# Layer scale on one core: y's big load moved to ACT's queue, x's tail cut 56 and 4, x's head rows last

## The chip, the cores and the metric

The kernel runs on one core of one Trainium2 chip. The time is the device time of one execution in microseconds, the median of several runs. The core has a matrix engine (PE), a vector engine (DVE), ACT, POOL and SP, and 16 DMA engines that move data between HBM and the on-chip memory (SBUF). SP and ACT each have a DMA queue; in this profile q1 is SP's and q10 is ACT's, and both use the same 16 DMA engines.

## The reference

```python
B, S, D = 1024, 16, 512
x, y:  normal(B, S, D) * 0.05, bf16
gamma: 1e-4 * normal(D) * 0.05, bf16

def reference(x, y, gamma):
    return x + gamma * y
```

Each of x, y and the output is 16384 rows of 512 bf16 values, 16.78 MB. So 33.56 MB are read and 16.78 MB written, and the arithmetic is one multiplication and one addition for each element.

## The kernel before

The 16384 rows are spread over 128 partitions, 128 rows of 1 KB to a partition. `BLOCKS` cuts these into three blocks of 4, 64 and 60 rows; inside a block a partition's rows lie next to each other in HBM, so that one transfer moves one unbroken run for each partition (64 KB for 64 rows). A whole y (128 KB for each partition) stays in SBUF and is turned into the output in place; x has room for 76 rows only, so its last 60 rows reuse room of earlier ones.

Nothing schedules the work: three lists at the head of the file write its order out by hand. `SP` and `ACT` are the DMA instructions of the two queues, in program order. `('y', a, b)` loads rows a to b of y, `('x', a, b, at)` loads rows of x to row `at` of x's room, `('g',)` loads gamma, `('s', a, b)` stores. `DVE` is the order of the arithmetic over the pieces of `PIECES` (8, 16, 44, 52 and 8 rows): `('m', c)` multiplies piece c of y by gamma (line 180), `('a', c)` adds x to it (line 189).

`ring` (lines 113 to 140) writes out a queue's list. Before a transfer it puts the waits that the transfer needs, and the issuing engine stands there until they are met, with all that follows in its list behind it:

- `EARLY` instructions (the first two of SP, the first of ACT) are moved to the very start of the program.
- At the position `AHEAD` each queue waits once until the transfer `HOLD`, y's rows 0 to 4, has landed. PE watches for that landing (line 147) and releases SP, ACT and DVE. So the load of x's rows 4 to 68 and of y's rows 68 to 128 on SP, and of gamma on ACT, are issued only then.
- A load of x into room that is in use waits until the additions that read it are done (`frees`). The load of x's rows 68 to 120 takes the room of rows 24 to 68 and waits for addition 2; that of rows 120 to 128 waits for addition 0, the second in DVE's order.
- The first store waits for `RELEASE`, the landing of x's rows 68 to 120 (line 157), and every store for its additions.

Gamma comes as one row of 1 KB. PE multiplies it by a column of ones (line 152), which copies it to 128 partitions, and DVE casts the result to `gamma_sb` (line 154). All multiplications read `gamma_sb`; they come after the cast on DVE. A multiplication also waits for its rows of y, an addition for its rows of x and for the multiplications before it. DVE's order is: multiply pieces 0, 1, 2; add 2, 0, 1; multiply 3, 4; add 3, 4.

Of the kernel before, what the change touches and what calls it, by code (L numbers as in the profile page):

```python
# [5 lines left out]

BLOCKS = [4, 64, 60]

PIECES = [8, 16, 44, 52, 8]


SP = [
    ('y', 0, 4),
    ('y', 4, 68),
    ('x', 4, 68, 4),
    ('y', 68, 128),
    ('x', 68, 120, 24),
    ('x', 120, 128, 0),
]
ACT = [('x', 0, 4, 0), ('g',), ('s', 4, 68), ('s', 0, 4), ('s', 68, 128)]  # L20

EARLY = (2, 1)

HOLD, AHEAD = ('y', 0, 4), (2, 1)

RELEASE = ('x', 68, 120, 24)

DVE = [('m', 0), ('m', 1), ('m', 2), ('a', 2), ('a', 0), ('a', 1), ('m', 3), ('m', 4), ('a', 3), ('a', 4)]
MULT, ADD = mybir.AluOpType.mult, mybir.AluOpType.add


def _take(sem, n, eng):


    return eng.wait_ge(sem, n).then_inc(sem, -n)  # L35


def kernel(
# [18 lines left out]
    rows = N // P  # L57
    n = len(PIECES)
    assert sum(PIECES) == rows
    starts = [sum(PIECES[:c]) for c in range(n + 1)]  # L60
    dt = xf.dtype
# [13 lines left out]
    y_sb = nc.alloc_sbuf_tensor("y_sb", [P, rows, D], dt).ap()  # L75
    x_loads = [w for w in ACT + SP if w[0] == "x"]
    y_loads = [w for w in SP + ACT if w[0] == "y"]
    stores = [w for w in SP + ACT if w[0] == "s"]
    for loads in (x_loads, y_loads, stores):
# [9 lines left out]
    s_add, s_go, s_rel, s_end, s_out = sem("s_add"), sem("s_go"), sem("s_rel"), sem("s_end"), sem("s_out")  # L89
    added = [a for kind, *a in DVE if kind == "a"]  # L90
    order = {a[0]: k for k, a in enumerate(added)}

    def meets(a, b, c, d):
        return a < d and c < b
# [4 lines left out]
    def x_at(row):  # L99
        return next(w[3] + row - w[1] for w in x_loads if w[1] <= row < w[2])  # L100
# [12 lines left out]
    def ring(eng, what, n_early, n_ahead):  # L113

        known, went = 0, False
        for k, w in enumerate(what):
            kind = w[0]
            if k == n_ahead:
                _take(s_held[eng], 1, eng)
            need = frees(w) if kind == "x" else pieces_of(w[1], w[2]) + list(w[3:]) if kind == "s" else []  # L120
            need = max((order[c] + 1 for c in need), default=0)
            if kind == "s" and not went:
                _take(s_go, 1, eng)
                went = True
            if need > known:
                eng.wait_ge(s_add, need)
                known = need
            if kind == "g":
                i = eng.dma_start(out=gamma_row, in_=gamma.unsqueeze(0)).then_inc(s_gamma, 16)
            elif kind == "x":  # L130
                to = x_sb[:, w[3] : w[3] + w[2] - w[1], :]
                i = eng.dma_start(out=to, in_=rows_of(xf, w[1], w[2])).then_inc(s_load[w], 16)
            elif kind == "y":
                r = slice(w[1], w[2])
                i = eng.dma_start(out=y_sb[:, r, :], in_=rows_of(yf, w[1], w[2])).then_inc(s_load[w], 16)
            else:
                r = slice(w[1], w[2])
                i = eng.dma_start(out=rows_of(of, w[1], w[2]), in_=y_sb[:, r, :]).then_inc(s_out, 16)
            if k < n_early:
                early.append(i.ins)  # L140

    ring(nc.sync, SP, EARLY[0], AHEAD[0])
    ring(nc.scalar, ACT, EARLY[1], AHEAD[1])

# [11 lines left out]

    _take(s_load[RELEASE], 16, nc.tensor)
    nc.tensor.sem_inc(s_go, 1)
# [4 lines left out]
    def need(loads, c):  # L163
        for w in loads:
            if w not in landed and meets(starts[c], starts[c + 1], w[1], w[2]):
                if w == RELEASE:
                    _take(s_rel, 1, nc.vector)
                elif w == HOLD:
                    _take(s_held[nc.vector], 1, nc.vector)
                else:  # L170
                    _take(s_load[w], 16, nc.vector)
                landed.add(w)

    for kind, *args in DVE:
        c = args[0]
        yt = y_sb[:, starts[c] : starts[c + 1], :]
        if kind == "m":
            need(y_loads, c)
            g = gamma_sb[:, None, :].to_broadcast([P, PIECES[c], D])
            nc.vector.tensor_tensor(out=yt, in0=yt, in1=g, op=MULT).then_inc(s_dve, 1)  # L180
            open_mults += 1
        else:
# [4 lines left out]
            at = x_at(starts[c])  # L187
            xt = x_sb[:, at : at + PIECES[c], :]
            nc.vector.tensor_tensor(out=yt, in0=xt, in1=yt, op=ADD).then_inc(s_add, 1)  # L189
# [44 lines left out]
```

## Time and profile before

| | us |
|---|---|
| time, median of 3 runs (119.63 to 119.88) | 119.76 |
| span of the profiled execution, first to last instruction | 118.2 |
| median time less this span | 1.5 |
| DVE busy in the span | 70.1 |
| gamma's DMA issued / matmul of gamma starts | 3.90 / 11.59 |
| first multiplication starts | 23.95 |
| addition 2 starts | 43.45 |
| load of x's rows 68 to 120 issued | 55.37 |
| first store issued | 77.41 |

The profiled execution's own device time is not on the page, only its span; the row below it is the difference to the median of the timed runs. The page gives times from the first instruction. A line of the timeline reads: start, duration, engine, line of the kernel, operation, what it writes and reads, how often, and in brackets how long the engine was idle before it and what it waited for. "SPq" and "ACTq" lines are the instructions that issue a DMA; the transfer itself goes on afterwards. In the row of 40 slices each digit is the busy share of the DMA engines in tenths. Besides, the trace holds a record of every DMA packet (queue, start, duration, bytes) and the time at which each of a transfer's 16 parts reports that it has landed; where the text gives a packet's or a landing's time, it is from these.

### The profile page before, as it was taken

The page shows a single profiled execution, that of the slowest core. Times are in us where ns is not written, and L with a number is a line of the kernel's source. Part 1 is how long each engine was busy: PE and PEld are TensorE (multiplying, and loading weights), DVE is VectorE, ACT ScalarE, POOL GpSimd, SP SyncE. Part 2 cuts the span into 40 slices and gives each one's busy share as a digit, 9 for nine tenths or more (in the row PEclk, how much of TensorE's full clock was granted, in tenths as well). Part 3 has the DMA queues.
Part 4 walks back from the last instruction along what each step waited for, and adds up shares of the span by engine and source line. Part 5 has one row for each costly group of instructions (what it writes and reads, how often), then busy time and mean ns, then how long its engine had stood idle before and what let it go on. Part 6 is the DMA issues. An engine that isn't in the chain of part 4 may idle for free. (4 is left out here: it accounts for less than half of the span.)

```text
span 118.2 us, 91 instructions
## 1 busy us (share of the span) xinstructions
PE 0.6 (0%) x1; PEld 0.1 (0%) x1; DVE 70.1 (59%) x12; POOL 0.2 (0%) x4
## 2 busy tenths in 40 slices
PE   0000100000000000000000000000000000000000
PEld 0000000000000000000000000000000000000000
DVE  0000200089999969999999999999999900000000
POOL 0000000000000000000000000000000000000000
DMA  6999889988899879879969696898899889799793
GB/s 248 461 666 399 355 355 399 665 355 355 355 599 466 355 333 624 374 333 499 499 288 576 288 576 288 360 637 355 355 576 488 355 355 510 333 582 416 333 499 166
DMA packets 1442, 50.33 MB, mean 426 GB/s; under 512 B 161, under 2 KB 162, under 8 KB 546
## 3 DMA queue, kind: packets, MB, share of 16 engines
q1 hardware_dynamic: 864, 33.03, 64.8%
q10 hardware_dynamic: 578, 17.30, 33.9%
HBM read 33.56 MB, written 16.78 MB: 426 GB/s over the span
## 5 line engine op out<-in xcount | busy, mean ns | idle before, releaser
L180 DVE TENSOR_TENSOR y_sb<-y_sb,gamma_sb 128x4096 bf16<-128x4096 bf16 (+3 forms) x5 | 34.7, 6981 | 10.9 <-DVEq L35 10.9
L189 DVE TENSOR_TENSOR y_sb<-x_sb,y_sb 128x4096 bf16<-128x4096 bf16 (+3 forms) x5 | 34.7, 6981 | 1.2 <-DVEq L35 1.1
L154 DVE CAST gamma_sb<-gamma_ps 128x512 bf16<-128x512 f32 x1 | 0.7, 692 | 10.2 <-DVEq L35 10.2
L146 DVE MEMSET ones_row<- 1x128 bf16 x1 | 0.2, 165 | 2.0 <-PEq L51 2.0
L152 PE MATMUL gamma_ps<-gamma_row,ones_row 1*128 1x512 bf16 x1 | 0.6, 581 | 11.6 <-PEq L35 11.6
L152 PEld LDWEIGHTS gamma_ps<-gamma_row,ones_row 1*128 1x128 bf16 x1 | 0.1, 101 | 11.6 <-issue 11.6
L218 POOL MEMSET const-bfloat16-1.0<- 128x1 bf16 x1 | 0.1, 101 | 0.0
L218 POOL MEMSET const-uint8-127<- 128x1 uint8 x1 | 0.1, 101 | 0.0
L218 POOL MEMSET const-float32-0.0<- 128x1 f32 x1 | 0.1, 98 | 0.2 <-issue 0.2
L218 POOL MEMSET const-float32-1.0<- 128x1 f32 x1 | 0.1, 98 | 0.0
## 6 DMA issues: line engine op xcount, KB each, us to landing
y_sb<-in_y_dram SPq DMA_DIRECT2D x1, 7680.0 KB, 57.3
out_dram<-y_sb ACTq DMA_DIRECT2D x1, 7680.0 KB, 23.8
x_sb<-in_x_dram SPq DMA_DIRECT2D x1, 6656.0 KB, 21.7
x_sb<-in_x_dram SPq DMA_DIRECT2D x1, 1024.0 KB, 22.0
y_sb<-in_y_dram SPq DMA_DIRECT2D x1, 512.0 KB, 3.4
x_sb<-in_x_dram ACTq DMA_DIRECT2D x1, 512.0 KB, 4.2
out_dram<-y_sb ACTq DMA_DIRECT2D x1, 512.0 KB, 22.3
y_sb<-in_y_dram SPq DMA_DIRECT2D x1, 23.4
```

What stands on the lines that cost most here:

```text
L146: nc.vector.memset(ones_row, 1.0).then_inc(s_ones, 1)
L152: nc.tensor.matmul(gamma_ps, ones_row, gamma_row, start=True, stop=True).then_inc(s_ps, 1)
L154: nc.vector.tensor_copy(out=gamma_sb, in_=gamma_ps).then_inc(s_dve, 1)
L180: nc.vector.tensor_tensor(out=yt, in0=yt, in1=g, op=MULT).then_inc(s_dve, 1)
L189: nc.vector.tensor_tensor(out=yt, in0=xt, in1=yt, op=ADD).then_inc(s_add, 1)
L218: nc = _bacc.Bacc("TRN2", target_bir_lowering=False, num_devices=1)
```

## The change

The five lists and numbers at the head of the file change, and nothing else.

- ACT's first instruction, still moved to the start, loads y's rows 4 to 68; it was SP's second. Gamma follows it on ACT's queue, as it followed x's rows 0 to 4. Only one instruction of SP is moved to the start now, y's rows 0 to 4.
- x's rows 0 to 4 are SP's last load. They take room of x's rows 4 to 8 and wait for addition 1.
- x's last 60 rows come as rows 68 to 124, which wait for addition 2 (rows 20 to 68), and 124 to 128, which have room of their own. The stores are released by the landing of rows 68 to 124.
- The pieces are 4, 16, 48, 56 and 4 rows. DVE adds piece 0 last instead of after piece 2, and the store of rows 0 to 4 is the last of the stores.

```diff
-PIECES = [8, 16, 44, 52, 8]
+PIECES = [4, 16, 48, 56, 4]
 
 SP = [
     ('y', 0, 4),
-    ('y', 4, 68),
-    ('x', 4, 68, 4),
+    ('x', 4, 68, 0),
     ('y', 68, 128),
-    ('x', 68, 120, 24),
-    ('x', 120, 128, 0),
+    ('x', 68, 124, 16),
+    ('x', 124, 128, 72),
+    ('x', 0, 4, 0),
 ]
-ACT = [('x', 0, 4, 0), ('g',), ('s', 4, 68), ('s', 0, 4), ('s', 68, 128)]
-
-EARLY = (2, 1)
-
-HOLD, AHEAD = ('y', 0, 4), (2, 1)
-
-RELEASE = ('x', 68, 120, 24)
-
-DVE = [('m', 0), ('m', 1), ('m', 2), ('a', 2), ('a', 0), ('a', 1), ('m', 3), ('m', 4), ('a', 3), ('a', 4)]
+ACT = [('y', 4, 68), ('g',), ('s', 4, 68), ('s', 68, 128), ('s', 0, 4)]
+
+EARLY = (1, 1)
+
+HOLD, AHEAD = ('y', 0, 4), (1, 1)
+
+RELEASE = ('x', 68, 124, 16)
+
+DVE = [('m', 0), ('m', 1), ('m', 2), ('a', 2), ('a', 1), ('m', 3), ('m', 4), ('a', 3), ('a', 4), ('a', 0)]
```

## The prediction

> **What bounds the kernel now.** I read the page's head first, then the slices of the span, the issues, and the timeline.
>
> ```profile
> span 118.2 us, 91 instructions
> PE 0.6 (0%) x1; PEld 0.1 (0%) x1; DVE 70.1 (59%) x12; POOL 0.2 (0%) x4
> ...
> DMA  6999889988899879879969696898899889799793
> DMA packets 1442, 50.33 MB, mean 426 GB/s; under 512 B 161, under 2 KB 162, under 8 KB 546
> ...
> q1 hardware_dynamic: 864, 33.03, 64.8%
> q10 hardware_dynamic: 578, 17.30, 33.9%
> ```
>
> DVE works for 59% of the span; the two DMA queues (q1 is SP's, q10 ACT's) take 98.7% of the 16 DMA engines' time. The records of single packets say the same from below. One packet is one partition's run of a transfer: 64 KB takes 2.42 us, 60 KB 2.27, 52 KB 1.97, 8 KB 0.309, 4 KB 0.159, and each engine has eight of every transfer. That is 3 x 19.36 (y 4-68, x 4-68, store 4-68) + 2 x 18.15 (y 68-128, store 68-128) + 15.73 + 2.47 (x's last 60 rows) + 3 x 1.27 = 116.4 us per engine. The first packet starts at 1.00 us and the last ends at 117.85: 0.45 us is idle. So nothing but DMA time or a new DMA gap can move the end, and a gain is at most some 0.4 us.
>
> The timeline shows what keeps the engines fed.
>
> ```profile
> 0.00 0.85 SPq L135 DMA_DIRECT2D y_sb<-in_y_dram  x2
> 0.13 0.38 ACTq L132 DMA_DIRECT2D x_sb<-in_x_dram  x1
> ...
> 3.71 0.33 SPq L132 DMA_DIRECT2D x_sb<-in_x_dram  x1
> 3.90 0.50 ACTq L129 DMA_DIRECT2D gamma_row<-in_gamma_dram  x1
> ...
> 11.59 0.58 PE L152 MATMUL gamma_ps<-gamma_row,ones_row 1*128 1x512 bf16 x1 [11.59 <-PEq L35]
> 12.32 0.69 DVE L154 CAST gamma_sb<-gamma_ps 128x512 bf16<-128x512 f32 x1 [10.16 <-DVEq L35]
> 23.95 18.43 DVE L180 TENSOR_TENSOR y_sb<-y_sb,gamma_sb 128x4096 bf16<-128x4096 bf16 x3 [10.94 <-DVEq L35]
> 43.45 18.43 DVE L189 TENSOR_TENSOR y_sb<-x_sb,y_sb 128x22528 bf16<-128x22528 bf16 x3 [1.08 <-DVEq L35]
> 55.37 2.53 SPq L132 DMA_DIRECT2D x_sb<-in_x_dram  x2
> ```
>
> Gamma is issued at 3.90 and lands at 11.45, alone in ACT's queue: its 1 KB starts at 8.62, when its engine has finished two more of SP's 64 KB packets, and its completion comes after one more. The first multiplication waits for y 4-68, not for gamma. The big addition (rows 24 to 68) ends at 55.34 and frees x's buffer; SP issues x's tail at 55.37. With 1.3 us from issue to packet (step 5) it could start at 56.7, and the engines run out of y 68-128 only from 60.5 on: 3.8 us of cover, no gap. That cover is what the change touches.
>
> **The change part by part.**
>
> *Small parts.* x's last 60 rows as 56 and 4 instead of 52 and 8: 8 x 2.12 (56 KB, between the 52 and 60 KB rows) + 1.27 = 18.2 us against 15.73 + 2.47 = 18.2: nothing. Head rows of x and the store of rows 0-4 moved last: the same packets elsewhere; while x's tail runs alone, 1.27 + 1.27 = 2.5 us of SP's packets follow it and cover the release of the stores (issue 77.41 to first store packet 78.73, 1.3 us), as x's 8 last rows do now (2.47). DVE: one piece of 4096 elements is gone, other sizes shift; of 70.1 us nothing is on the end.
>
> *Step 1: y 0-4 lands later.* In the trace ACT's first packets start at 2.21, when SP's y 0-4, running since 1.00 to 1.38, has 5.2 to 7.6 of 8 packets done on an engine. From there the packets of both queues alternate; one engine shows SP, ACT, SP, ACT at 2.08, 2.25, 2.40, 2.56. Now ACT's are of 4 KB, then of 64 KB: each remaining turn of y 0-4, and its completion, stands behind one of 2.42 us. With no delay it lands at 3.38 as now; with three packets left at about 2.4 + 4 x 2.42 + 0.35 = 12.4. I take one left on the slowest engine (turns: packet, completion): 2.4 + 2 x 2.42 + 0.35 = 7.6.
>
> *Step 2: x 4-68 starts.* PE's release puts it 0.33 us behind (3.38 to 3.71). From gamma's row, issue to first packet against a queue of 64 KB packets is 4.7 us (3.90 to 8.62). So S, the time from which the queues share, is 7.6 + 0.3 + 4.7 = 12.6. Bounds: 3.38 + 0.3 + 1.3 = 5.0 and 17.4.
>
> *Step 3: gamma now stands behind y 4-68.* It is ACT's second transfer, so its packet starts after the eight of 64 KB on its engine. At S the engines, busy since about 1.2, have 1.2 + 1.27 + 19.36 - S = 9.2 us of y left, and alternating with x doubles it: y's data end at 12.6 + 18.4 = 31.0. Then y's completion, gamma and gamma's completion each wait for one packet of x, as gamma's completion does now (8.67 to 11.1): 3 x 2.42 + 0.35. Gamma lands at 38.6. In general that is 51.3 - S: 46 for S = 5.0, 34 for 17.4, and up to 4.8 earlier if two of the three turns fall away.
>
> [...]
>
> *Step 4: the DVE chain.* From gamma's landing to the first multiplication 1.8 us (11.45, cast done 13.01, its wait to 13.18). Three multiplications of rows 0-68: 18.43, the same 68 rows. The addition of 48 rows: 11.89 x 48/44 = 12.97. Sum 33.2: it ends at 71.8 where it ended at 55.34. Both orders run these back to back, and x 4-68 has landed long before (all of y 0-4, y 4-68 and x 4-68 by about 44).
>
> *Step 5: the gap.* SP issues x's 56 rows at 71.8, first packet 1.3 later, as the first store's: 73.1. What was issued before is 1.27 + 19.36 + 19.36 + 18.15 = 58.1 us from 1.2, gone at 59.3. Behind SP's wait stand x 124-128 and x 0-4, and ACT's stores wait for the 56 rows: nobody else has work. The engines idle for 13.8 us.
>
> *Sum.* From 73.1: 16.94 + 2.54 + 19.36 + 18.15 + 1.27 + 0.35 = 58.6, end 131.7. The store of 68-128 needs the additions of 56 and 4 rows: 71.8 + 4.4 + 15.1 + 1.2 + 15.1 + 1.2 = 108.8, first packet 110.1; the store of 4-68, from about 92.6, runs to 112.0. It fits by 2 us. The span is 131.7 instead of 118.2, plus 13.5. The median of the runs, 119.76, is 1.5 above the profiled span; with the same around it: 133.2.
>
> **The rivals.**
>
> *A, the forecast, with its spread.* End = 144.3 - S in span, so 139.3 for S = 5.0 and 126.9 for 17.4; with two turns fewer, 4.8 less. Times 125 to 141. Chance 0.86.
>
> *B, y 0-4 loses almost every turn.* If ACT's descriptors reach the engines first (the two issues lie only 0.13 us apart), all eight packets of y 0-4 alternate with those of y 4-68 and it lands at 1.2 + 1.27 + 19.36 + 0.35 = 22.2. Then x and gamma are issued at 22.5, with 2.0 us of idle engines until 23.8; gamma, nearly unrivalled, lands at 24.3 to 28.7, the addition ends at 57.5 to 61.9, x's tail starts at 58.8 to 63.2 against loads that last to 61.3. Loss 2.0 to 3.9: 121.8 to 123.7. Against it: SP's first packet is at 1.00, ACT's at 2.21. Chance 0.07.
>
> *C, not slower: the engines finish y 4-68 before they turn to x.* Gamma would land near 22.5, the addition would end at 55.7 and x's tail be there by 57.0, before 59.3. This decides wherever gamma lands before 59.3 - 1.3 - 33.2 = 24.8. Then 119.8, 0.3 either way. Against it, gamma's own turn at 8.62 and the alternation at 2.2 to 2.6. Chance 0.05.
>
> *D, none of these,* 0.02.
>
> **How the numbers follow.** The time is A's, 133.2. A's own range is 125 to 139 with 0.05 of its 0.86 outside; B, C and D lie below, 0.14. That leaves out 0.19, so 125 to 139 is the range. About 0.2% (0.24 us) is what a measurement of this kernel can tell from no change. C gives mostly the same: same 0.04. Faster by more needs C and most of the 0.45 us of idle engines: 0.02. Slower 0.94.
>
> **What would show it.** Step 1: y 0-4's landing at 7.6 (5 to 12.4) and x 4-68's issue 0.3 behind. Steps 2 and 3: y 4-68 landing past 30 instead of 23.8, gamma's matmul near 38.7 instead of 11.59. Step 4: the first multiplication near 40.4, idle before it put down to gamma's chain, the addition's end near 71.8. Step 5: a hole of some 14 us in the DMA row from 59, DMA work after it unchanged, and DVE busy still about 70. It is wrong if the matmul comes before 23: then no hole opens and the two times are alike.

## The result, and the profile after

The changed kernel takes 135.07 us (134.96 to 135.37, four runs) against 119.72 for the kernel before (119.63 to 119.88, four runs): 1.1283 times as long, 95% interval 1.1267 to 1.1299. The profiled span is 133.6 us instead of 118.2.

The page of the changed kernel first: span, busy times, the DMA row and the queues.

```profile
span 133.6 us, 91 instructions
PE 0.6 (0%) x1; PEld 0.1 (0%) x1; DVE 70.1 (52%) x12; POOL 0.2 (0%) x4
...
DMA  9799797797996969660000979696978979899993
...
q1 hardware_dynamic: 864, 25.17, 44.4%
q10 hardware_dynamic: 578, 25.17, 43.6%
```

The bytes and DVE's 70.1 us are those of before. What is new is the four zeros in the DMA row: slices of 3.3 us in which the engines move almost nothing, called the hole below. The queues' shares add up to 88% instead of 98.7%, since the span has grown round the same traffic.

The timeline of the changed kernel shows what the engines wait for.

```profile
0.00 0.37 SPq L135 DMA_DIRECT2D y_sb<-in_y_dram  x1
0.12 0.38 ACTq L135 DMA_DIRECT2D y_sb<-in_y_dram  x1
...
8.71 0.33 SPq L132 DMA_DIRECT2D x_sb<-in_x_dram  x1
8.91 0.50 ACTq L129 DMA_DIRECT2D gamma_row<-in_gamma_dram  x1
9.09 0.42 SPq L135 DMA_DIRECT2D y_sb<-in_y_dram  x1
...
39.47 0.58 PE L152 MATMUL gamma_ps<-gamma_row,ones_row 1*128 1x512 bf16 x1 [39.47 <-PEq L35]
40.19 0.69 DVE L154 CAST gamma_sb<-gamma_ps 128x512 bf16<-128x512 f32 x1 [38.36 <-DVEq L35]
41.14 18.43 DVE L180 TENSOR_TENSOR y_sb<-y_sb,gamma_sb 128x2048 bf16<-128x2048 bf16 x3 [0.26 <-DVEq L35]
59.72 17.29 DVE L189 TENSOR_TENSOR y_sb<-x_sb,y_sb 128x24576 bf16<-128x24576 bf16 x2
72.71 4.66 SPq L132 DMA_DIRECT2D x_sb<-in_x_dram  x3
```

Gamma's matmul moved from 11.59 to 39.47, and everything that needs gamma moved with it. DVE now waits 38.4 us for the cast; after that its work runs without a break. Addition 2 ends at 72.68 and SP can issue the rest of x only at 72.71.

Three stretches of the changed kernel, as rows of start and end, length, busy time (and count) of PE, PEld, DVE and POOL, clock, busy share of the DMA engines, GB/s:

```profile
1.00:60.00 59.00, 0.58 (x1) 0.10 (x1) 19.57 (x6) 0.00 (x0) 1.00 0.99 427
60.00:74.00 14.00, 0.00 (x0) 0.00 (x0) 14.00 (x2) 0.00 (x0) 1.00 0.14 45
74.00:133.60 59.60, 0.00 (x0) 0.00 (x0) 36.52 (x6) 0.00 (x0) 1.00 0.96 412
```

Before the hole the engines are 99% busy, after it 96%. In the hole DVE works all 14 us: the loads are through, and the next load waits for DVE. By the packet records no engine has a packet from 60.06 to 73.66. In the kernel before, the same stretch was full:

```profile
60.00:74.00 14.00, 0.00 (x0) 0.00 (x0) 14.00 (x2) 0.00 (x0) 1.00 0.98 426
```

The records also close the account. Averaged over the 16 engines, idle time between the first and the last packet is 14.85 us (0.43 before), and the packets themselves take 117.68 us (116.72 before). That is 14.4 + 1.0 = 15.4 us, the whole difference of the spans.

### The profile page after: what moved, and what is told of

Read it like the earlier page. It is cut to its first block, busy times and chain, and to the rows that moved or that the text cites. A ratio compares the mean times of both kernels' runs of the same rounds, so it can differ in the third digit from the quotient of the medians.

```text
span 133.6 us, 91 instructions
## 1 busy us (share of the span) xinstructions
PE 0.6 (0%) x1; PEld 0.1 (0%) x1; DVE 70.1 (52%) x12; POOL 0.2 (0%) x4
## 5 line engine op out<-in xcount | busy, mean ns | idle before, releaser
L189 DVE TENSOR_TENSOR y_sb<-x_sb,y_sb 128x2048 bf16<-128x2048 bf16 (+3 forms) x5 | 34.7, 6981 | 0.3
L180 DVE TENSOR_TENSOR y_sb<-y_sb,gamma_sb 128x2048 bf16<-128x2048 bf16 (+3 forms) x5 | 34.7, 6981 | 0.3 <-DVEq L35 0.3
L154 DVE CAST gamma_sb<-gamma_ps 128x512 bf16<-128x512 f32 x1 | 0.7, 691 | 38.4 <-DVEq L35 38.4
## 6 DMA issues: line engine op xcount, KB each, us to landing
out_dram<-y_sb ACTq DMA_DIRECT2D x1, 7680.0 KB, 22.8
out_dram<-y_sb ACTq DMA_DIRECT2D x1, 512.0 KB, 22.9
y_sb<-in_y_dram ACTq DMA_DIRECT2D x1, 34.9
```

The source lines that it names most:

```text
L154: nc.vector.tensor_copy(out=gamma_sb, in_=gamma_ps).then_inc(s_dve, 1)
```

## The experiments

Three rivals were to be told apart from the theory of the forecast. The forecast says: an engine serves the two queues one packet in turn, so gamma, queued behind y 4-68, and y 4-68 itself come late as soon as x 4-68 shares the engines; DVE is late by as much, and SP cannot issue x's tail. One rival puts the loss on ACT's queue or on the move as such, another on a single part of this (gamma's place alone, or y's lateness alone), a third on the other edits. The column "us" is the median of the runs; each ratio in the text is to the kernel before measured beside that run (119.77 to 119.81). The other times in the table are read from the profiles; "idle" is the engines' mean idle time between first and last packet.

| kernel | us | first big packet of x 4-68 | y 4-68 landed | gamma landed | x's tail issued | idle |
|---|---|---|---|---|---|---|
| before | 119.72 | (behind y) | 23.8 | 11.5 | 55.4 | 0.4 |
| changed | 135.07 | 12.3 | 35.0 | 39.3 | 72.7 | 14.9 |
| the rest only | 119.90 | (behind y) | 22.8 | 12.8 | 55.3 | 0.5 |
| swap in the kernel before | 119.94 | 23.3 | 23.9 | 23.9 | 56.3 | 0.5 |
| x 0-4 second | 120.62 | 23.3 | 23.8 | 23.7 | 57.1 | 1.1 |
| gamma early, hold on y | 122.68 | 24.2 | 22.9 | 15.3 | 58.3 | 2.6 |
| hold on y | 126.09 | 24.1 | 22.8 | 30.2 | 63.6 | 5.2 |
| x 4-68 in halves | 126.77 | 12.4 | 29.0 | 31.1 | 64.5 | 6.6 |
| gamma on SP | 127.92 | 12.4 | 34.9 | 15.2 | 65.4 | 8.0 |
| x 4-68 early | 137.63 | 10.0 | 37.5 | 41.9 | 75.3 | 17.6 |
| y 4-68 in halves | 149.01 | 9.8 | 49.1 | 53.2 | 86.6 | 28.8 |

### The other parts without the move

```diff
     ('y', 0, 4),
+    ('y', 4, 68),
     ('x', 4, 68, 0),
...
-ACT = [('y', 4, 68), ('g',), ('s', 4, 68), ('s', 68, 128), ('s', 0, 4)]
+ACT = [('g',), ('s', 4, 68), ('s', 68, 128), ('s', 0, 4)]
-EARLY = (1, 1)
+EARLY = (2, 0)
-HOLD, AHEAD = ('y', 0, 4), (1, 1)
+HOLD, AHEAD = ('y', 0, 4), (2, 0)
```

> The change without the move: y 4-68 stays SP's second transfer and gamma is alone on ACT's queue, the pieces, x's tail of 56 and 4, x 0-4 last and the order of stores as changed. Forecast's theory (these parts cost nothing): 119.7 us, at most 0.4 either way. Rival 'some of the 15 us belongs to these parts' (the changed kernel's end lies 1.9 us later than the forecast's sum): 120.5 to 122 us.

It took 119.90 us, ratio 1.0008 (0.9998 to 1.0017): no difference to the kernel before. As long as y 4-68 stays on SP's queue, the pieces, the cut of x's tail, x's head rows at the end and the order of the stores cost nothing; the 15 us do not come without the move. Whether the move brings them by itself is the next question.

### The move without the other parts: the swap in the kernel before

```diff
     ('y', 0, 4),
-    ('y', 4, 68),
+    ('x', 0, 4, 0),
     ('x', 4, 68, 4),
...
-ACT = [('x', 0, 4, 0), ('g',), ('s', 4, 68), ('s', 0, 4), ('s', 68, 128)]
+ACT = [('y', 4, 68), ('g',), ('s', 4, 68), ('s', 0, 4), ('s', 68, 128)]
```

> The kernel before, with y 4-68 on ACT's queue and x 0-4 in its place on SP's, nothing else. Forecast's theory (an engine gives each queue one packet in turn): SP's nine or ten remaining turns of y 0-4 and x 0-4 are packets of 4 KB, so x 4-68, behind them, meets y 4-68 only when that is nearly through (S near 20 to 22 instead of 12.6). y 4-68 lands near 23 to 25, gamma between 24 and 30, the hole is 0 to 3 us: 119.7 to 123 us. Rival 'the move of y 4-68 to ACT's queue with gamma behind it costs the 15 us by itself': 134 to 136 us.

119.94 us, ratio 1.0013 (1.0004 to 1.0022). Here too y 4-68 is ACT's first load with gamma behind it, and it costs 0.15 us. The timeline of this kernel:

```profile
8.93 0.50 ACTq L129 DMA_DIRECT2D gamma_row<-in_gamma_dram  x1
...
24.00 0.58 PE L152 MATMUL gamma_ps<-gamma_row,ones_row 1*128 1x512 bf16 x1 [24.00 <-PEq L35]
...
56.28 2.53 SPq L132 DMA_DIRECT2D x_sb<-in_x_dram  x2
```

Gamma lands 12.4 us later than in the kernel before and it does not matter: it arrives with y 4-68, and x's tail is issued 0.9 us later than before, inside the cover. So the move alone is not the cause either: it costs 15 us only together with another part of the change. The part that the forecast's theory names is the place of x 0-4. Here SP has it in front of x 4-68, and its 4 KB packets take SP's turns until y 4-68 is through (first packet of x 4-68 at 23.3, y 4-68 landed at 23.9); in the changed kernel it comes last. The next run changes only this, and with it the room that x's 4 last rows take.

### The same inside the changed kernel

```diff
     ('y', 0, 4),
+    ('x', 0, 4, 72),
     ('x', 4, 68, 0),
     ('y', 68, 128),
     ('x', 68, 124, 16),
-    ('x', 124, 128, 72),
-    ('x', 0, 4, 0),
+    ('x', 124, 128, 0),
```

> The changed kernel, but x 0-4 comes as SP's second load, after the hold and ahead of x 4-68, and the 4 last rows of x take the reused room instead. Forecast's theory (turns by packet): from about 12.3 eight packets of 4 KB and a completion take SP's turns beside y's four remaining packets of 64 KB, so y's data end near 22.2 to 23 and x 4-68 starts with them; gamma lands at 24 to 28, addition 2 ends at 57.3 to 61.3, the hole is 0 to 2.5 us: 119.7 to 122.5 us. Rival 'what counts is that y 4-68 and gamma share ACT's queue': 134 to 136 us.

120.62 us, ratio 1.0067 (1.0053 to 1.008). Eight packets of 4 KB for each engine, put in front of x 4-68, take 14.45 of the 15.35 us away. Gamma landed at 23.7, just ahead of the expected 24 to 28: the turns in front of it were now of 4 KB. The timeline of this kernel:

```profile
23.84 0.58 PE L152 MATMUL gamma_ps<-gamma_row,ones_row 1*128 1x512 bf16 x1 [23.84 <-PEq L35]
...
57.08 4.66 SPq L132 DMA_DIRECT2D x_sb<-in_x_dram  x2
```

The hole in front of x's tail is gone altogether: the tail's first packet starts at 60.77, as the first engine ends its last packet of y 68-128. Most of the 0.9 us that remain lie later: no engine has a packet from 79.47 to 79.88, and between 78 and 82 an engine idles 0.8 us on the mean, against none between 76 and 82 in the kernel before. x 0-4 no longer follows the tail here, so less stands behind it while the first store is released; the kernel with the rest only, where x 0-4 follows, has no such gap.

### x 4-68 earlier

```diff
-EARLY = (1, 1)
+EARLY = (2, 1)
-HOLD, AHEAD = ('y', 0, 4), (1, 1)
+HOLD, AHEAD = ('y', 0, 4), (2, 1)
```

> The changed kernel, but x 4-68 is issued at the start, as SP's second instruction, so that it does not wait for y 0-4's landing. Forecast's theory: x's packets stand directly behind y 0-4's completion and the sharing begins one turn earlier, at S = 9.9 instead of 12.3; by the forecast's end = 144.3 - S everything is 2.4 us later, gamma lands near 41.7: 137.5 us. Rival 'the late release after the hold is what costs': faster than 135.

137.63 us against the expected 137.5, with x's first packet at 10.0 and gamma at 41.9. Issuing a load 8 us earlier makes the kernel 2.6 us slower, because the earlier load takes turns from the one that matters: y 4-68 landed at 37.5 instead of 35.0.

### Whose packets are smaller

x 4-68 in halves:

```diff
-    ('x', 4, 68, 0),
+    ('x', 4, 36, 0),
+    ('x', 36, 68, 32),
```

> The changed kernel, but x 4-68 comes as two transfers of 32 rows, 32 KB packets instead of 64 KB, back to back on SP's queue. Forecast's theory (turns by packet, whatever its size): from 12.3 on, y's four remaining packets stand behind one of 1.21 us each instead of 2.42, so y's data end near 26.9, gamma lands near 30.7 instead of 39.3, addition 2 ends at 64.1 and the hole is some 5.2 us instead of 13.8: 126.5 us. Rival 'the engines share by bytes or by time': y and gamma land as before and it stays at 135.

y 4-68 in halves:

```diff
-ACT = [('y', 4, 68), ('g',), ('s', 4, 68), ('s', 68, 128), ('s', 0, 4)]
-EARLY = (1, 1)
-HOLD, AHEAD = ('y', 0, 4), (1, 1)
+ACT = [('y', 4, 36), ('y', 36, 68), ('g',), ('s', 4, 68), ('s', 68, 128), ('s', 0, 4)]
+EARLY = (1, 2)
+HOLD, AHEAD = ('y', 0, 4), (1, 2)
```

> The changed kernel, but y 4-68 comes as two transfers of 32 rows on ACT's queue, 32 KB packets against x's 64 KB. Forecast's theory (turns by packet): y 0-4 lands at about 5.2, x starts near 8, y's eleven remaining half packets stand behind x's eight of 2.42 us and then behind packets of 60 KB; y ends near 49, gamma lands near 56, addition 2 ends near 89 and the hole is some 30 us: 147 to 154 us. Rival 'the engines share by bytes or by time': 135 us.

126.77 and 149.01 us, where sharing by bytes or by time expects 135 for both. Halving x's packets brings gamma from 39.3 to 31.1, halving y's puts it at 53.2 (expected near 56). The hole, in the kernel with y in halves:

```profile
60.00:87.50 27.50, 0.00 (x0) 0.00 (x0) 27.35 (x4) 0.00 (x0) 1.00 0.00 0
```

So, in these runs, an engine gave each queue one packet in turn, and the size of its packets set a queue's share: y 4-68 landed at 35.0 against x in 64 KB, at 29.0 against x in 32 KB, and at 49.1 when its own were of 32 KB.

### Gamma alone: on SP's queue

```diff
     ('y', 0, 4),
+    ('g',),
     ('x', 4, 68, 0),
...
-ACT = [('y', 4, 68), ('g',), ('s', 4, 68), ('s', 68, 128), ('s', 0, 4)]
+ACT = [('y', 4, 68), ('s', 4, 68), ('s', 68, 128), ('s', 0, 4)]
```

> The changed kernel, but gamma goes on SP's queue, after y 0-4 and before x 4-68, instead of behind y 4-68 on ACT's. Forecast's theory: gamma lands near 15, the sharing of the engines is unchanged, y 4-68 still lands near 35.0, and now y is what the second multiplication waits for. That multiplication starts at 35.1, addition 2 ends 4.3 + 12.95 + 12.97 later at 65.4, x's 56 rows start at 66.4, the hole shrinks from some 13.8 to 6.5: 127.9 us. Rival 'gamma's place in the queue is the whole cause': the hole closes, 119.8 us. Rival 'y's delay is the whole cause': nothing changes, 135.

127.92 us. Both single causes fall: gamma's place is worth 7.15 us, the rest is y's own lateness. The timeline of this kernel shows DVE waiting in another place (its lines are numbered one higher, since the list at the head is one line longer):

```profile
15.34 0.58 PE L153 MATMUL gamma_ps<-gamma_row,ones_row 1*128 1x512 bf16 x1 [15.34 <-PEq L36]
16.07 0.69 DVE L155 CAST gamma_sb<-gamma_ps 128x512 bf16<-128x512 f32 x1 [14.24 <-DVEq L36]
17.01 1.23 DVE L181 TENSOR_TENSOR y_sb<-y_sb,gamma_sb 128x2048 bf16<-128x2048 bf16 x1 [0.26 <-DVEq L36]
35.01 17.29 DVE L181 TENSOR_TENSOR y_sb<-y_sb,gamma_sb 128x8192 bf16<-128x8192 bf16 x2 [16.77 <-DVEq L36]
```

Gamma is ready at 17, and the second multiplication stands for 16.8 us until y 4-68 has landed at 34.9.

### No sharing: the hold on y 4-68, and with gamma early

The hold on y 4-68:

```diff
-HOLD, AHEAD = ('y', 0, 4), (1, 1)
+HOLD, AHEAD = ('y', 4, 68), (1, 1)
```

> The changed kernel, but SP and ACT are held until y 4-68 has landed, not y 0-4, so that x 4-68 cannot share the engines with y 4-68; gamma stays on ACT's queue behind y 4-68. Forecast's theory (sharing makes both y and gamma late): y lands near 22.2, x and gamma are issued at 22.5, the engines idle some 2 us, gamma lands at 24.3 to 28.7, addition 2 ends at 57.6 to 62.0: 121.8 to 124.5 us. Rival 'ACT's queue itself serves y 4-68 or gamma slowly, whoever shares': gamma still lands past 33 and the time stays above 130.

126.09 us: the mechanism as expected (y landed at 22.8), the size missed by 1.6. The rival falls: gamma landed before 33 and the time is below 130. The timeline:

```profile
23.14 0.33 SPq L132 DMA_DIRECT2D x_sb<-in_x_dram  x1
23.34 0.50 ACTq L129 DMA_DIRECT2D gamma_row<-in_gamma_dram  x1
...
30.36 0.58 PE L152 MATMUL gamma_ps<-gamma_row,ones_row 1*128 1x512 bf16 x1 [30.36 <-PEq L35]
```

Gamma landed at 30.2, not at 28.7 at the latest. The engines stood empty from 22.49 to 24.09, and the first 64 KB packet of x then took 2.6 to 3.4 us instead of 2.42; gamma stood behind it, and its completion behind one more. So addition 2 ended at 63.6, not at 62.0 at the latest, and a second hole, from 62.66 to 64.56, stands in front of x's tail.

With gamma as SP's second transfer at the start as well:

```diff
     ('y', 0, 4),
+    ('g',),
     ('x', 4, 68, 0),
...
-ACT = [('y', 4, 68), ('g',), ('s', 4, 68), ('s', 68, 128), ('s', 0, 4)]
+ACT = [('y', 4, 68), ('s', 4, 68), ('s', 68, 128), ('s', 0, 4)]
-EARLY = (1, 1)
+EARLY = (2, 1)
-HOLD, AHEAD = ('y', 0, 4), (1, 1)
+HOLD, AHEAD = ('y', 4, 68), (2, 1)
```

> The changed kernel with both causes taken away: gamma is issued at the start as SP's second transfer, and x 4-68 is held until y 4-68 has landed. Forecast's theory: gamma lands before 12, y 4-68 near 22 to 23, the multiplications run as in the kernel before, x 4-68 lands near 43.5, addition 2 ends near 56.3 and x's tail is in time; what is left is one hole of some 2 us while x is issued: 121 to 122.5 us. Rival 'something else in the changed kernel costs time, too': above 123 us.

122.68 us, 0.2 above the expected range. Gamma landed at 15.3, not before 12, which cost nothing, and the one hole is left: 2.6 us idle in all, and 0.9 us more packet time than before (117.62 against 116.72). With both causes gone, what remains is these two.

No run was faster than the kernel before, whose engines idle 0.43 us.

## Why the prediction was right

The forecast of 133.2 us was 1.9 too low, within 125 to 139. By its own steps:

- *What bounds it.* Right. The time differs by idle DMA time and packet time and by nothing else.
- *Small parts.* Right for what the forecast priced, the packets: the kernel with these alone took 119.90 us. What it did not see is that one of them decides the price of the move: with x 0-4 in front of x 4-68 instead of at the end, the changed kernel took 120.62. And no piece is gone, as it says: there are five before and after, and the two of 4096 elements became two of 2048; DVE's 70.1 us are the same.
- *Step 1.* y 0-4 landed at 8.38 (7.6 expected), and SP issued x 0.33 later as expected. The last packet of 4 KB on each engine went out behind one packet of 64 KB (from 4.90 to 5.50) and the completion behind a second (from 7.47 to 8.07), as assumed.
- *Step 2.* S, 12.6 in the forecast: the first packet of x 4-68 starts at 12.32. That it is so close is partly luck: y 0-4 landed 0.8 later than assumed, and from x's issue to its first packet it took 3.6 us (8.71 to 12.32), not 4.7. The two misses cancel.
- *Step 3.* y's data end at 32.2 (31.0) and gamma lands at 39.33 (38.6). From 12.3 on the records alternate, one packet of 64 KB from each queue. The kernels with halved packets show that turns go by packet (gamma at 31.1 and 53.2 instead of 39.3).
- *Step 4.* 33.35 us from gamma's landing to the end of addition 2, against 33.2.
- *Step 5.* The hole lasts from 60.06 to 73.66, expected 59.3 to 73.1. The first packet came 0.95 us after the issue, not 1.3.
- *The sum* is where the missing 1.9 us lie. Gamma was 0.7 late and the chain after it 0.15, the issue gave 0.35 back. From 73.66 to the end it took 60.0 us instead of the 58.6 summed, and of these 1.4 us the packets of x's 56 rows are a half: 17.63 us for each engine instead of 16.94, because the first one after the hole took 2.2 to 3.2 us, mostly 2.8, and not 2.12. Most of the rest is idle time: 0.26 us for each engine because they restarted not together but from 73.66 to 74.46, and 0.43 in the last 0.8 us, in which one engine after another ran out of work.
- *The rivals.* B (y 0-4 losing nearly every turn) did not come about in this kernel, but the run with x 0-4 second has its mechanism: the small packets on SP's queue held up what stood behind them (x 4-68's first packet at 23.3 instead of 12.3) and left the engines to ACT's (y 4-68 landed at 23.8 instead of 35.0). B's price was too low: the hold on y 4-68 issues x at 23.1, near B's 22.5, and took 126.09 us, not 121.8 to 123.7, with gamma at 30.2 instead of 28.7 at the latest. C (engines finish y 4-68 first) is refuted by the alternating records and the halved packets. That ACT's load might reach the engines first was not tried.
- *The range.* Its lower end, 125, is neither of the ends that the forecast's own formula gives (126.9 + 1.5 = 128.4, or 123.6 with two turns fewer).

A turn in these runs is one packet, 64, 32 or 60 KB in the big transfers: with data waiting on both queues, the eight packets that an engine has of such a transfer never went out in one turn. In the changed kernel the engines send x 4-68 and y 4-68 in turn from 12.32 to 32.2, a packet taking 2.42 us in the median.

The cause needs two edits together, y 4-68 on ACT's queue and no small load in front of x 4-68 on SP's. What it then costs has two halves which the run with gamma on SP parts: 7.15 us for gamma behind a large load on its queue, and 8.2 us for the large load itself sharing the engines with one that is needed later (127.92 - 119.72). The halves are those of this order: with the sharing taken away first, by the hold on y 4-68, 8.98 us go, although that kernel has 1.6 us of empty engines of its own.

## What to carry to other kernels

With the DMA engines 99% busy, putting a load on a second queue did not add speed here; it gave half the turns to something else, and the load that the first compute step needs came later (y 4-68 landed at 35.0 instead of 23.8). Before a load is moved, ask what stands behind it on its new queue (here 1 KB on which all arithmetic waits) and how much cover the next buffer release has (here 3.8 us against a delay of 17). In these runs the size of its packets set the share of a queue (y 4-68 landed at 49.1 in 32 KB packets, at 35.0 in 64 KB), and a small transfer in front of a large one kept the large one back (x 4-68's first packet at 23.3 instead of 12.3).

## What was not expected of the hardware

- The first packet after an empty stretch was slower: 56 KB took 2.2 to 3.2 us instead of 2.12 after the hole of 13.6 us, 64 KB 2.6 to 3.4 instead of 2.42 after one of 1.6 us. Both holes thus cost some 0.7 us more than their length; in all seven kernels with a hole in front of a load the first packets after it took 0.6 to 0.8 us longer on the mean. What delays the packet, no run shows.
- From issue to first packet on empty engines it took 0.95 us in both cases (72.71 to 73.66, 23.14 to 24.09), and 0.95 to 0.98 after the other holes in front of loads.
- The trace's packet records name no engine. The chains of packets quoted here join each packet to the engine that ended one just then; where several end together, two engines can be confused.
